# Which streams may reserve an engine, and when the dense-layer weights are loaded: a change to a list-scheduled two-layer kernel

## The chip, the cores and the metric

The kernel runs on one core of one Trainium2 chip. The metric is the time of one execution on the device in microseconds (us), as the median of several runs. The kernel before takes 727.18 us (three runs, 726.22 to 729.38). All runs compared here are of the state "fast"; the one slow run, of l_gap3, is named where it comes up. A ratio is the mean time of one kernel's fast runs over the mean of the other kernel's fast runs of the same rounds, so it is not quite the ratio of the medians quoted beside it.

Engine names: PE is TensorE, PEld its weight loads, DVE is VectorE, ACT is ScalarE, POOL is GpSimd, SP is SyncE, which here only issues DMAs.

## The reference, cut to what matters

Two layers, each an attention with a memory followed by a dense layer; 2048 tokens, width 640, 32 heads of 20, and a hidden width of 1728. The attention works in four segments of 512 tokens; each segment adds to a memory `M` that the next one reads.

```python
x = A_x
x = x + _A_ref(_layernorm(x), wq, wk, wv, wo, beta)   # attention, layer 1
x = x + _B_ref(_layernorm(x), w1, w2)                 # dense layer 1: relu(x @ w1) @ w2
x = x + _A_ref(_layernorm(x), wq, wk, wv, wo, beta)   # attention, layer 2 (same weights)
x = x + _B_ref(_layernorm(x), w1, w2)                 # dense layer 2
# in _A_ref, for each segment s and head:
#   p = softmax(q k^T * scale + causal mask);  a_dot = p v
#   a_mem = phi(q) M / (phi(q) z + 1e-6);      o = g a_mem + (1 - g) a_dot
#   M += phi(k)^T v;  z += sum phi(k)
```

## The kernel before: the parts that matter

The program is not written in its final order. Each part of the computation is a *stream*, a Python generator that yields operations. A list scheduler, run when the program is built, models each engine's time and decides the order in which each engine gets its instructions. That order is then fixed in the program, and an instruction whose input is not there yet waits on a semaphore. In the traces of before the 6344 matmuls follow, stream by stream, the order in which the scheduler put them.

```python
S.add(0, items(scores));  S.add(1, items(apply));  S.add(2, each(out_proj))
S.add(3, each(fill));     S.add(3, each(spill));   S.add(4, each(memory))
S.add(5, each(proj));     S.add(6, each(ffn))      # ffn: the dense layers, lowest compute stream
S.add(7, consts());       S.add(8, loads());       S.add(8, late_loads())
```

`scores` and `apply` treat four heads at a time; I call that a head group, 8 in a segment, 64 in all.

At each step the scheduler takes, of all streams' next operations, the one that can start first. Before that it applies a *reservation*: an operation is refused if a stream with a smaller priority number has a next operation on the same engine that could start before this one would end, beyond a tolerance.

```python
HOLD_TOL = {"pe": 220.0, "act": 150.0, "dve": 200.0, "pool": 0.0, "sp": 0.0}   # ns
...
for prio, n, st, alts in heads:                  # alts: (end, start, k, engine)
    ok = []
    for end, start, k, e in alts:
        if not any(p2 < prio and any(e2 == e and s2 + HOLD_TOL[e] < end for _, s2, _, e2 in al2[:1])
                   for p2, _, _, al2 in heads):
            ok.append((end, start, k))
```

PSUM has eight banks. Four belong to the scores (`X`, `Y`), one to apply (`OD`), and three (`MISC`) to everything else: projections, output projection, memory and dense layers. A matmul group can start only if one of the three is free; the bank comes free when an ACT or DVE operation has read it.

```python
MISC = [Slot(ps[:, 5 + k, :], "misc%d" % k) for k in range(3)]
...
def evac(n, mode, vfn, afn, waits=(), psum=True):            # reader on ACT or on DVE
    return Op([("act", (52.0 if psum else 94.0) + n / 1.2, [(afn, True)], 125.0),
               ("dve", 66.0 + n / (0.96 * mode), [(vfn, True)], 95.0)], waits)
...
def add_half(t, hf, bk, tk, waits=()):                       # residual add, DVE only
    ta = yield dve(320, 1, lambda e: e.tensor_tensor(
        x_sb[...], x_sb[...], bk.ap[:, 0:320], ALU.add), [tk] + list(waits))
    bk.release(ta)                                           # the bank comes free here
```

Q and K go through DRAM to be laid out by head: `spill` writes `scr` from `stg`, `fill` reads `pad` from `scr`. POOL issues the large loads at once:

```python
def late_loads():
    xt = yield Need("xt0")                       # first transposed activations
    ...                                          # x1, x2, x3, then wo
    z1 = yield Need("z1")
    ...                                          # w1 in one DMA of 2.2 MB, w2 in two, together 2.2 MB
```

The softmax here doesn't subtract the row's maximum and nothing guards it: scores larger than these inputs give would overflow.

Of the kernel before, what the change touches and what calls it, by code (L numbers as in the profile page):

```python
# [12 lines left out]
DH = 20  # L13
NSEG = 4
L = T // NSEG
DFF = 1728
TT = T // 128
FC = D // 128
# [6 lines left out]
NFULL = DFF // 128  # L25
# [13 lines left out]
class Prog:  # L39
# [44 lines left out]
    def dma(self, e, fn, sem):  # L84
        self.pos[e] += 1
        self.dcnt[id(sem)] = self.dcnt.get(id(sem), 0) + 16
        tk = (sem, self.dcnt[id(sem)])
        self.ops[e].append(("op", fn, sem, 16))
        self.info[(id(sem), tk[1])] = ("dma%d" % id(sem), tk[1], dict(self.K[e]))
        return tk  # L90
# [53 lines left out]

SEM_NS = 60.0
PE_MARGIN = 80.0
HOLD_TOL = {"pe": 220.0, "act": 150.0, "dve": 200.0, "pool": 0.0, "sp": 0.0}


class Sched:  # L150
# [54 lines left out]
    def _alts(self, op):  # L205
# [7 lines left out]
        for k, (e, hold, fns, tail) in enumerate(op.alts):  # L213
            m = PE_MARGIN if e == "pe" else 0.0
            start = max([self.at(t) + SEM_NS + m for t in waits], default=0.0)
# [4 lines left out]
    def run(self):  # L220
        while True:
            best = None
            moved = True
            while moved:
                moved = False
                for st in self.streams:
                    had = st[2]
                    self._settle(st)
                    if st[2] is not had and not isinstance(st[2], Op):
                        moved = moved or st[2] is None  # L230
            heads = [(st[0], n, st, self._alts(st[2])) for n, st in enumerate(self.streams)
                     if not st[4] and isinstance(st[2], Op)]
            for prio, n, st, alts in heads:
                ok = []
                for end, start, k, e in alts:
                    if not any(p2 < prio and any(e2 == e and s2 + HOLD_TOL[e] < end for _, s2, _, e2 in al2[:1])
                               for p2, _, _, al2 in heads):
                        ok.append((end, start, k))
                if not ok:
                    continue  # L240
                end, start, k = min(ok)
                key = (round(start), prio, n)
                if best is None or key < best[0]:
                    best = (key, st, end, start, k)
            if best is None:
                stuck = [st for st in self.streams if not st[4]]
                if not stuck:
                    return
                raise RuntimeError("stuck: " + "; ".join(
                    str(getattr(st[2], "key", None) or [s.name for s in st[2].slots][:2]) for st in stuck))  # L250
            _, st, end, start, k = best
            op = st[2]
            e, hold, fns, tail = op.alts[k]
            waits, slot = op.waits, None
            if op.acq is not None:
                slot = self._pick(op.acq)
                slot.free = False
                waits = waits + slot.tks
                fns = [(lambda eng, fn=fn, slot=slot: fn(eng, slot), mark) for fn, mark in fns]
            self.P.waits(e, waits)  # L260
            self.free[e] = end
            if op.dma is not None:
                tk = self.P.dma(e, fns[0][0], op.dma)
                self.dma_free[e] = max(self.dma_free[e], end) + tail[1]
                self.t[(id(tk[0]), tk[1])] = self.dma_free[e] + tail[0]
                out = tk
            else:
                marks = []
                for fn, mark in fns:
                    tk = self.P.op(e, fn, mark)  # L270
                    if tk is not None:
                        self.t[(id(tk[0]), tk[1])] = end + tail
                        marks.append(tk)
                out = marks[0] if len(marks) == 1 else (marks or None)
            st[2], st[3] = None, ((slot, out) if slot is not None else out,)
# [31 lines left out]
def bass_interleave_layers__memory_aug_infini_attn__dense_activation_relu__prompt_kernel(  # L307
    nc, A_x, A_wq, A_wk, A_wv, A_wo, A_beta, B_x, B_w1, B_w2, out,
):
    with contextlib.ExitStack() as es:  # L310
        sb = lambda name, shape, dtype=dt.bfloat16: es.enter_context(nc.sbuf_tensor(name, shape, dtype))
        sem_ = lambda name: es.enter_context(nc.semaphore(name))
        P = Prog({e: sem_("clk_" + e) for e in ["act", "dve", "pool", "pe"]})
        S = Sched(P)
# [7 lines left out]
        w1_r = sb("w1_r", [128, FC, DFFP])  # L322
        w2_r = sb("w2_r", [128, NDC, D])
# [9 lines left out]
        x_sb = sb("x_sb", [128, TT, D])  # L333
# [29 lines left out]
        pad_sem = {id(s): sem_("pad%d" % k) for k, s in enumerate(PAD)}  # L363
        scr = nc.dram_tensor("scr", [2, D + 12, 2 * L], dt.bfloat16, kind="Internal").ap()
        scr_sem = [[sem_("scr%d_%d" % (n, c)) for c in range(FC)] for n in range(2)]
# [17 lines left out]
        def ld(e, name, nbytes, fn, waits=()):  # L383
            tk = yield dma(e, sem_("d_" + name), nbytes, fn, waits)
            S.set(name, tks=[tk])

        def wload(e, name, w, src, waits=()):
            yield from ld(e, name, 819200, lambda eng: eng.dma_start(
                w[:], src.rearrange("(c p) d -> p c d", p=128)), waits)

        xs = A_x[0].rearrange("(t p) d -> p t d", p=128)
# [7 lines left out]
            yield from wload("sp", "wv", wv_r, A_wv)  # L399

        def late_loads():
            xt = yield Need("xt0")
            for s in range(1, NSEG):
                yield from ld("pool", "x%d" % s, 655360, lambda e, s=s: e.dma_start(
                    x_sb[:, 4 * s:4 * s + 4, :], xs[:, 4 * s:4 * s + 4, :]), xt if s == 1 else [])
            yield from wload("pool", "wo", wo_r, A_wo)
            z1 = yield Need("z1")
            yield from ld("pool", "w1", 2211840, lambda e: e.dma_start(
                w1_r[:, :, 0:DFF], B_w1.rearrange("(c p) f -> p c f", p=128)), z1)
            s2 = sem_("d_w2")  # L410
            yield dma("pool", s2, 2129920, lambda e: e.dma_start(
                w2_r[:, 0:NFULL, :], B_w2[0:NFULL * 128, :].rearrange("(c p) d -> p c d", p=128)))
            tk = yield dma("pool", s2, 81920, lambda e: e.dma_start(
                w2_r[0:DFF - NFULL * 128, NFULL, :], B_w2[NFULL * 128:DFF, :]), z1)
            S.set("w2", tks=[tk])
# [164 lines left out]
        def spill(a, s):  # L580
            for c in range(FC):
                ev = yield Need("stg", a, s, c)
                before = S.events.get(("filled", a, s - 2) if s > 1 else ("filled", a - 1, s + 2), [])
                tk = yield dma("sp", scr_sem[s % 2][c], 262144, lambda e, c=c: e.dma_start(
                    scr[s % 2, 128 * c:128 * c + 128, :], stg[:, c].rearrange("p n t -> p (n t)")),
                    ev + before, issue=700.0)
                S.set("packed", a, s, c, tks=[tk])

        def fill(a, s):
            got = []  # L590
            for g in range(G):
                sl = yield Acq(PAD)
                w = yield Need("z2")
                w = list(w)
                for c in range(80 * g // 128, min(FC - 1, (80 * g + 91) // 128) + 1):
                    t = yield Need("packed", a, s, c)
                    w += t
                row = scr[s % 2, 80 * g:80 * g + 1, :]
                tk = yield dma("sp", pad_sem[id(sl)], 262144, lambda e, sl=sl, row=row: e.dma_start(
                    sl.ap.rearrange("p n t -> p (n t)"),  # L600
                    bass.AP(tensor=row.tensor, offset=row.offset,
                            ap=[[DH * 2 * L, 4], [2 * L, 32], [1, 2 * L]])), w + sl.tks, issue=800.0)
                S.set("pad", a, s, g, tks=[sl, tk])
                got.append(tk)
            S.set("filled", a, s, tks=got)
# [277 lines left out]
        S.add(1, items(apply))  # L883
        S.add(2, each(out_proj))
        S.add(3, each(fill))
        S.add(3, each(spill))
        S.add(4, each(memory))
        S.add(5, each(proj))
        S.add(6, each(ffn))
        S.add(7, consts())  # L890
        S.add(8, loads())
        S.add(8, late_loads())
        S.run()
        P.waits("sp", [S.last])
# [31 lines left out]
```

## Time and profile before

| stretch, us | 0–46 | 46–120 | 120–300 | 300–480 | 480–640 | 640–722 |
|---|---|---|---|---|---|---|
| PE idle, us (length minus PE busy) | 34.4 | 19.9 | 15.3 | 17.0 | 20.2 | 4.9 |

The page's first and second part, for the kernel before. The first line gives busy time, share of the span and number of instructions. In the rows below each digit is a tenth of busy time (or of the granted TensorE clock) in one of 40 equal slices:

```profile
PE 610.5 (85%) x6344; PEld 340.6 (47%) x6344; DVE 399.6 (55%) x1178; ACT 427.5 (59%) x599; POOL 175.1 (24%) x278
PE   0644968988889999798998989897699897999998
...
PEclk9966976999999999999999889998799999999999
DMA  5958226255425233630237401255012430040201
```

The windows view, for the three middle stretches; the first number after the stretch is its length, then each engine's busy time with its number of instructions, then granted clock, DMA share and GB/s:

```profile
120.00:300.00 180.00, 164.74 (x1935) 89.48 (x1934) 121.39 (x365) 138.57 (x197) 55.25 (x86) 0.99 0.40 85
300.00:480.00 180.00, 163.05 (x1738) 90.66 (x1735) 104.80 (x299) 122.21 (x168) 50.21 (x79) 0.94 0.29 66
480.00:640.00 160.00, 139.85 (x1503) 79.67 (x1504) 91.20 (x262) 87.56 (x120) 35.93 (x57) 0.93 0.29 61
```

PE is the busiest engine, and it has one long hole at the start. The chain that ended last (start, length, what) shows a slow spill and a very slow fill, and the timeline of PE shows that PE waited for that fill:

```profile
23.70 7.46 DMA scr<-stg
31.18 14.98 DMA pad<-scr
```

```profile
29.56 1.03 PE L469 MATMUL ps<-xnT,wk_r 128*128 128x512 bf16 x4
46.21 0.61 PE L733 MATMUL ps<-pad 20*128 20x512 bf16 x4 [15.62 <-DMA pad<-scr]
```

In 28–44 us the DMA engines' share is 0.98: POOL issued about 7 MB at 19–25 us.

Here is the timeline of PE and then of DVE near 505 us, at the end of a segment:

```profile
504.96 0.34 PE L645 MATMUL ps<-BD,stg 128*128 128x147 bf16 x3
511.17 0.50 PE L645 MATMUL ps<-BD,stg 128*128 128x84 bf16 x3 [5.87 <-DVE o_sb L657]
```

### The profile page before, as it was taken

The page shows a single profiled execution, that of the slowest core. Times are in us where ns is not written, and L with a number is a line of the kernel's source. Part 1 is how long each engine was busy: PE and PEld are TensorE (multiplying, and loading weights), DVE is VectorE, ACT ScalarE, POOL GpSimd, SP SyncE. Part 2 cuts the span into 40 slices and gives each one's busy share as a digit, 9 for nine tenths or more (in the row PEclk, how much of TensorE's full clock was granted, in tenths as well). Part 3 has the DMA queues.
Part 4 walks back from the last instruction along what each step waited for, and adds up shares of the span by engine and source line. Part 5 has one row for each costly group of instructions (what it writes and reads, how often), then busy time and mean ns, then how long its engine had stood idle before and what let it go on. Part 6 is the DMA issues. An engine that isn't in the chain of part 4 may idle for free.

```text
span 722.3 us, 15107 instructions
## 1 busy us (share of the span) xinstructions
PE 610.5 (85%) x6344; PEld 340.6 (47%) x6344; DVE 399.6 (55%) x1178; ACT 427.5 (59%) x599; POOL 175.1 (24%) x278
## 2 busy tenths in 40 slices
PE   0644968988889999798998989897699897999998
PEld 0223444443445644365445554354444455465645
DVE  5116486778668484346756566365764576434102
ACT  0326895888678678666897367680287756603140
POOL 0503332323323333223333123130132223200000
PEclk9966976999999999999999889998799999999999
DMA  5958226255425233630237401255012430040201
GB/s 164 365 210 136 83 98 136 74 114 99 112 76 80 26 49 122 103 74 5 38 112 125 65 1 39 95 107 99 1 37 104 95 76 19 11 92 18 60 15 37
DMA packets 99244, 60.90 MB, mean 84 GB/s; under 512 B 80040, under 2 KB 84568, under 8 KB 99176
## 3 DMA queue, kind: packets, MB, share of 16 engines
q1 hardware_dynamic: 97552, 52.67, 31.9%
q0 software_dynamic: 1408, 7.21, 2.7%
q8 instruction: 50, 0.82, 0.5%
q14 instruction: 18, 0.15, 0.1%
q10 hardware_dynamic: 216, 0.06, 0.0%
HBM read 27.11 MB, written 13.16 MB: 56 GB/s over the span
## 4 chain that ended last, share of the span: by engine, by line
PE 62%; DMA 17%; DVE 12%; ACT 7%; issue 1%; SPq 0%
PE ps L469 40%; PE ps L466 9%; DMA scr<-stg 8%; PE ps L733 6%; PE ps L768 6%; ACT PT L740 5%; DMA pad<-scr 3%; DMA phk<-phs 3%; DVE stats L477 2%; PE ps L687 2%; DMA oT<-o_sb 1%; DVE o_sb L657 1%; DMA xnT<-xn_tok 1%; DVE x_sb L802 1%; ACT stg L554 1%
## 5 line engine op out<-in xcount | busy, mean ns | idle before, releaser
L740 ACT ACTIVATE PT<-ps 128x1024 bf16<-128x1024 f32 (+1 forms) x384 | 317.9, 882 | 164.5 <-PE ps L733 163.9
L747 POOL TENSOR_SCALAR_AFFINE_SELECT PT<-PT 128x512 bf16<-128x512 bf16 x256 | 164.3, 654 | 433.7 <-ACT PT L740 433.7
L469 PE MATMUL ps<-w_r,hT 128*128 128x320 bf16 x832 | 137.2, 306 | 0.0
L802 DVE TENSOR_TENSOR x_sb<-x_sb,ps 128x320 bf16<-128x320 bf16 x128 | 61.2, 484 | 126.1 <-PE ps L469 126.0
L469 PE MATMUL ps<-xnT,w_r 128*128 128x512 bf16 x448 | 128.0, 382 | 0.0
L733 PE MATMUL ps<-pad 20*128 20x512 bf16 (+3 forms) x1024 | 72.4, 315 | 44.7 <-ACT PT L740 26.5
L469 PEld LDWEIGHTS ps<-w_r,hT 128*128 128x128 bf16 x832 | 80.7, 100 | 34.5 <-issue 3.3
L847 ACT ACTIVATE hT<-ps 128x512 bf16<-128x512 f32 x79 | 46.8, 600 | 59.5 <-PE ps L469 59.1
L768 PEld LDWEIGHTS ps<-v_aug,PT 128*128 128x128 bf16 x2560 | 73.7, 97 | 12.1 <-POOL PT L747 3.1
L768 PE MATMUL ps<-v_aug,PT 128*128 128x21 bf16 x2560 | 75.0, 173 | 1.5 <-issue 0.4
L733 PEld LDWEIGHTS ps<-pad 20*128 20x128 bf16 x1024 | 20.8, 92 | 108.0 <-ACT PT L740 41.6
L469 PEld LDWEIGHTS ps<-xnT,w_r 128*128 128x128 bf16 x448 | 43.1, 98 | 44.3 <-issue 3.0
L477 DVE BATCH_NORM_STATS2 stats<-x_sb 128x6 f32<-128x320 bf16 x128 | 54.5, 466 | 4.5 <-DMA x_sb<-in_A_x_dram 4.5
L469 PE MATMUL ps<-wo_r,oT 128*128 128x320 bf16 x256 | 50.9, 313 | 0.0
L554 ACT ACTIVATE stg<-ps 128x512 bf16<-128x512 f32 x51 | 30.5, 601 | 33.7 <-PE ps L469 33.5
L469 PE MATMUL ps<-wv_r,xnT 128*128 128x320 bf16 x256 | 48.3, 305 | 0.0
L469 PE MATMUL ps<-xnT,wq_r 128*128 128x512 bf16 x160 | 46.9, 407 | 0.0
L466 PE MATMUL ps<-xnT,w_r 128*128 128x512 bf16 x112 | 42.9, 383 | 4.0 <-issue 1.1
L469 PE MATMUL ps<-xnT,wk_r 128*128 128x512 bf16 x160 | 45.8, 395 | 0.0
L777 DVE RECIPROCAL rden<-ps 128x16 f32<-128x16 f32 x64 | 16.2, 253 | 50.8 <-PE ps L768 50.4
L627 ACT ACTIVATE stg<-stg 128x512 bf16<-128x512 bf16 x60 | 38.3, 638 | 9.4 <-DVE rtmp L625 9.2
L625 DVE TENSOR_SCALAR rtmp<-stg 128x512 bf16<-128x512 bf16 x60 | 22.5, 375 | 35.8 <-DMA scr<-stg 35.8
(65 smaller groups left out, 565.8 us busy)
## 6 DMA issues: line engine op xcount, KB each, us to landing
pad<-scr SPq DMA_DIRECT2D x64, 256.0 KB
scr<-stg SPq DMA_DIRECT2D x40, 256.0 KB, 4.3
out_dram<-x_sb SPq DMA_DIRECT2D x16, 160.0 KB, 1.8
w_r<-in_B_w_dram POOLq DMA_DIRECT2D x1, 2160.0 KB, 15.0
w_r<-in_B_w_dram POOLq DMA_DIRECT2D x1, 2080.0 KB, 20.0
x_sb<-in_A_x_dram POOLq DMA_DIRECT2D x3, 640.0 KB, 6.6
wk_r<-in_A_wk_dram SPq DMA_DIRECT2D x1, 800.0 KB, 7.3
wq_r<-in_A_wq_dram SPq DMA_DIRECT2D x1, 800.0 KB, 8.9
```

Of the source, the lines that this page charges most:

```text
L466: bk, tk = yield pe(mm_ns(n), [(lambda e, bk, a=a, b=b: e.matmul(bk.ap[:, 0:n] if len(b.shape) == 2 else bk.ap[:, 0:n].rearrange("p (i n) ...
L469: tk = yield pe(mm_ns(n), [(lambda e, k=k, a=a, b=b, bk=bk: e.matmul(bk.ap[:, 0:n] if len(b.shape) == 2 else bk.ap[:, 0:n].rearrange("p (i ...
L477: tk = yield dve(320, 1, lambda e, c2=c2: e.bn_stats(stats6[:, t, c2, :], x_sb[:, t, c2 * 320:(c2 + 1) * 320]), xt)
L554: lambda e, sg=sg, bk=bk: e.activation(sg.ap, bk.ap[:, :], ACT.Copy),
L625: tr = yield dve(512, 4, lambda e, rt=rt, q=q: e.tensor_scalar(rt.ap, q, 0.0, 1.0, ALU.max, ALU.add), p + rt.tks)
L627: te = yield act(512, lambda e, q=q: e.activation(q, q, ACT.Exp), [tr] + p, psum=False)
L733: fns.append((lambda e, j=j, hh=hh, N=N, o=o: e.matmul(ps[:, hh, o:o + N], sl.ap[32 * hh:32 * hh + DH, 0, 128 * j:128 * j + 128], sl.ap[32 ...
L740: tx = yield act(2 * w, lambda e, k=k, bkp=bkp, u=u, w=w: e.activation(pt.ap[:, 2 * k:2 * k + 2, PT_AT[u]:PT_AT[u] + w], bkp.ap[:, :, 0:w] ...
L747: tm = yield pool(600.0, lambda e, reg=reg: e.affine_select(out=reg, in_=reg, pattern=[[0, 4], [1, 128]], compare_op=ALU.is_ge, fill=0.0, ...
L768: fns.append((lambda e, i=i, hh=hh, j=j: e.matmul(od[:, i, hh, :], pt.ap[:, hh, PT_OFF[j] + 128 * (i - j):PT_OFF[j] + 128 * (i - j) + 128] ...
L802: ta = yield dve(320, 1, lambda e: e.tensor_tensor(x_sb[:, t, 320 * hf:320 * hf + 320], x_sb[:, t, 320 * hf:320 * hf + 320], bk.ap[:, 0:32 ...
L847: lambda e, dc=dc, bk=bk: e.activation(hT[:, dc, :], bk.ap[:, :], ACT.Relu), [tk] + HT.tks)
```

## The change: intent and diff

The description says that the scheduler "reserves engines only for scores and apply" and that the dense-layer weights are loaded "in pieces behind the first heads' progress". There are three parts. I name them H (holders), L (loads) and D (the modelled cost of spill and fill DMAs).

```diff
+HOLDERS = 1                                                                  # H
-                    if not any(p2 < prio and any(...
+                    if not any(p2 < min(prio, HOLDERS) and any(...

         def late_loads():                                                    # L (cut)
-            ... x1, x2, x3, wo, w1 and w2 one behind the other after xt0
+            w = yield Need("xt0");          yield from x_load(1, w)
+            w = yield Need("filled", 0, 0); yield from x_load(2, w)
             yield from wload("pool", "wo", wo_r, A_wo)
+            for k in range(FC):             # five pieces of w1
+                w = yield Need("o", k)      # head group k is done
+                tk = yield dma("pool", s1, 442368, ... B_w1[128 * k:128 * k + 128, :]), w + z1)
+            yield from x_load(3, [])
+            for n, kn in ((5, 4), (6, 8), (7, NFULL)):      # w2 behind head groups 5 to 7
+                w = yield Need("o", n)
+                yield dma("pool", s2, 163840 * (kn - k), ...)

-    spill: dma("sp", ..., 262144, ..., issue=700.0)                          # D
+    spill: dma("sp", ..., 400000, ..., issue=350.0)
-    fill:  dma("sp", ..., 262144, ..., issue=800.0)
+    fill:  dma("sp", ..., 400000, ..., issue=550.0)
```

With `HOLDERS = 1` only priority 0, the scores, reserves; the words "and apply" would need 2. The byte counts in D are only the scheduler's figures; the DMAs move what they moved before.

More of the change, by code (lines that the diff above doesn't have):

```diff
@@ L235, in run @@
                 for end, start, k, e in alts:
-                    if not any(p2 < prio and any(e2 == e and s2 + HOLD_TOL[e] < end for _, s2, _, e2 in al2[:1])
+                    if not any(p2 < min(prio, HOLDERS) and any(e2 == e and s2 + HOLD_TOL[e] < end for _, s2, _, e2 in al2[:1])
                                for p2, _, _, al2 in heads):
@@ L401, in late_loads, with x_load @@
         def late_loads():
-            xt = yield Need("xt0")
-            for s in range(1, NSEG):
-                yield from ld("pool", "x%d" % s, 655360, lambda e, s=s: e.dma_start(
-                    x_sb[:, 4 * s:4 * s + 4, :], xs[:, 4 * s:4 * s + 4, :]), xt if s == 1 else [])
+            def x_load(s, w):
+                yield from ld("pool", "x%d" % s, 655360, lambda e: e.dma_start(
+                    x_sb[:, 4 * s:4 * s + 4, :], xs[:, 4 * s:4 * s + 4, :]), w)
+            w = yield Need("xt0")
+            yield from x_load(1, w)
+            w = yield Need("filled", 0, 0)
+            yield from x_load(2, w)
             yield from wload("pool", "wo", wo_r, A_wo)
             z1 = yield Need("z1")
-            yield from ld("pool", "w1", 2211840, lambda e: e.dma_start(
-                w1_r[:, :, 0:DFF], B_w1.rearrange("(c p) f -> p c f", p=128)), z1)
-            s2 = sem_("d_w2")
-            yield dma("pool", s2, 2129920, lambda e: e.dma_start(
-                w2_r[:, 0:NFULL, :], B_w2[0:NFULL * 128, :].rearrange("(c p) d -> p c d", p=128)))
+            s1, s2 = sem_("d_w1"), sem_("d_w2")
+            for k in range(FC):
+                w = yield Need("o", k)
+                tk = yield dma("pool", s1, 442368, lambda e, k=k: e.dma_start(
+                    w1_r[:, k, 0:DFF], B_w1[128 * k:128 * k + 128, :]), w + z1)
+            S.set("w1", tks=[tk])
+            yield from x_load(3, [])
+            k = 0
+            for n, kn in ((5, 4), (6, 8), (7, NFULL)):
+                w = yield Need("o", n)
+                yield dma("pool", s2, 163840 * (kn - k), lambda e, k=k, kn=kn: e.dma_start(
+                    w2_r[:, k:kn, :], B_w2[128 * k:128 * kn, :].rearrange("(c p) d -> p c d", p=128)), w)
+                k = kn
             tk = yield dma("pool", s2, 81920, lambda e: e.dma_start(
@@ L583, in spill @@
                 before = S.events.get(("filled", a, s - 2) if s > 1 else ("filled", a - 1, s + 2), [])
-                tk = yield dma("sp", scr_sem[s % 2][c], 262144, lambda e, c=c: e.dma_start(
+                tk = yield dma("sp", scr_sem[s % 2][c], 400000, lambda e, c=c: e.dma_start(
                     scr[s % 2, 128 * c:128 * c + 128, :], stg[:, c].rearrange("p n t -> p (n t)")),
-                    ev + before, issue=700.0)
+                    ev + before, issue=350.0)
                 S.set("packed", a, s, c, tks=[tk])
@@ L598, in fill @@
                 row = scr[s % 2, 80 * g:80 * g + 1, :]
-                tk = yield dma("sp", pad_sem[id(sl)], 262144, lambda e, sl=sl, row=row: e.dma_start(
+                tk = yield dma("sp", pad_sem[id(sl)], 400000, lambda e, sl=sl, row=row: e.dma_start(
                     sl.ap.rearrange("p n t -> p (n t)"),
                     bass.AP(tensor=row.tensor, offset=row.offset,
-                            ap=[[DH * 2 * L, 4], [2 * L, 32], [1, 2 * L]])), w + sl.tks, issue=800.0)
+                            ap=[[DH * 2 * L, 4], [2 * L, 32], [1, 2 * L]])), w + sl.tks, issue=550.0)
                 S.set("pad", a, s, g, tks=[sl, tk])
```

## The prediction

> **What bounds the kernel now.** The page shows a span of 722.3 us with PE busy 610.5 us (85%), ACT 59%, DVE 55%, POOL 24%; the chain that ended last is 62% PE, 17% DMA. By stretches (the windows view) PE is idle 34 us of the first 46, 20 of 46–120, 15 of 120–300, 17 of 300–480, 20 of 480–640, and 5 in the tail 640–722, which is dense layer only.
>
> The largest reachable hole is at the start. After the first projections PE stops at 30.6 and resumes at 46.2 us: the timeline gives 15.6 us "<- DMA pad<-scr". The chain shows why: the first spill (scr<-stg) takes 7.46 us from 23.70, the first fill (pad<-scr) 14.98 us from 31.18. The DMA view's median for a spill is 4.3 us. In 20–43 us the DMA share is 1.0 at 340–420 GB/s, because POOL issued at 19–25 us all remaining x, wo, w1 and w2 (about 7 MB). The Trainium skill ("DMA: Bandwidth & Descriptors", "Issuing engines are not separate DMA queues") says that DMAs of all issuers share 16 engines and interleave; this trace agrees. The first dense-layer matmul runs only at 153 us: 4.3 MB came 100 us too early.
>
> **What the change does.**
> 1. Loads: only x1 (0.65 MB) stays ahead of the first spill; x2 and wo wait for the first segment's fills, w1 comes in five pieces behind heads 0–4, w2 behind heads 5–7. First spill about 3.5–4.5 us, first fill about 4: scores start at 31–34 us instead of 46. PE then has work at once (V projection, last Q chunk: 8 us at 46.8–55.6). Gain about 13 us. Also the clock: 0.50 in 36–48 us; the skill ("TensorE: Matmul & The Clock Gate", Part 1) tells of a half-rate state after idle windows. About 1 us more.
> 2. Cost: about 8 more POOL DMA issues of 0.6–1.1 us (trace: 0.58–1.15) among the masks (0.65 us each), POOL 24% busy: at most 1–2 us. w1/w2 now share the DMA engines with fills and transposes at 60–110 us, where the phk transpose already takes 11.2 us: 0–4 us lost.
> 3. Scheduler: with HOLDERS = 1 only priority 0, the scores, reserves an engine (the title's "and apply" does not follow from p2 < 1). PE operations hardly change (their length, about 216 ns, is under the 220 ns tolerance); lower work fills DVE, ACT and SP earlier, apply's DVE steps may come up to 0.5 us late, with about 8.9 us per head group to absorb that. The model's spill and fill issue (700/800 to 350/550 ns) now fits the trace (326/532 ns), and longer transfers push dependent PE work later, which should shorten in-order stalls on oT (8.6 us), phk (8.4 us) and DVE. I estimate 0–8 us gain, give or take 5 us.
>
> **Critical path.** PE has a nearly fixed sum of work, and leftover dense work sits in the tail, so idle removed at the start reaches the end almost whole. Sum: −13 −1 +3 −5 and about −4 of steadier filling: 707 us, range 696–719.
>
> **What would show it.** Right: DMA share well under 1 in 28–43 us; first score matmul by 34 us; PE idle of 0–46 us down by 10 or more; POOL issues spread to about 110 us; first dense matmul 10 us earlier; tail unchanged. Wrong: the first fill still above 8 us; new PE waits on w1/w2 or on masks; longer phk and fill transfers at 60–120 us; more idle after 120 us.
>
> **What would make it wrong.** In-order engines: POOL waiting for late o events delays masks; the new order losing more in mid-kernel than 13 us.

## More of the kernel before

Layer-norms belong to the stream that needs them: the one before a dense layer to `out_proj` (priority 2), the one before a projection to `proj` (5).

A stream offers one operation at a time, so while its next operation is refused, nothing behind it in that stream is offered either.

```profile
504.42 0.49 DVE L802 TENSOR_TENSOR x_sb<-x_sb,ps 128x320 bf16<-128x320 bf16 x1 [0.28 <-PE ps L469]
504.82 0.88 DVE L477 BATCH_NORM_STATS2 stats<-x_sb 128x6 f32<-128x320 bf16 x2
505.62 0.16 DVE L654 TENSOR_SCALAR rmem<-ps 128x16 f32<-128x16 f32 x1
...
508.95 0.17 DVE L487 TENSOR_SCALAR lnU<-mv 128x4 f32<-128x4 f32 x1
...
510.63 0.48 DVE L657 TENSOR_TENSOR o_sb<-ps,rmem 128x320 bf16<-128x320 f32 x1
...
514.62 0.48 DVE L802 TENSOR_TENSOR x_sb<-x_sb,ps 128x320 bf16<-128x320 bf16 x1
```

A dense-layer matmul group ended at about 505.0 us and its bank waited until 514.6 us for the residual add. Until 510.7 us DVE did a whole layer-norm of priority 2: eight `BATCH_NORM_STATS2`, then a chain of ten or so tiny dependent steps; after that came steps of memory and apply (priorities 4 and 1). A memory reader of another bank waited too, until 510.6 us. PE started nothing from 505.3 us until that reader had freed its bank.

## The result, and the profile after

The kernel after takes 686.74 us (median of three, 684.72 to 686.8) against 727.18. The ratio is 0.943, 95% interval 0.9387 to 0.9472. It is outside the forecast range: 20 us faster than forecast, with a gain of 40 us where 20 were forecast.

The same views of the kernel after:

```profile
PE 597.6 (87%) x6344; PEld 335.3 (49%) x6344; DVE 394.6 (58%) x1191; ACT 422.6 (62%) x586; POOL 179.2 (26%) x284
PE   0863953889998999999999999977998799999998
...
PEclk9985885899999999999999999998999999999999
DMA  5568459542661515280424502564023810050201
```

```profile
120.00:300.00 180.00, 169.68 (x1972) 93.15 (x1969) 124.77 (x385) 137.15 (x190) 56.84 (x87) 0.98 0.46 94
300.00:480.00 180.00, 170.87 (x1932) 97.36 (x1929) 113.92 (x331) 129.40 (x176) 54.03 (x84) 0.97 0.36 78
480.00:640.00 160.00, 151.74 (x1555) 86.78 (x1553) 90.22 (x273) 90.05 (x125) 35.05 (x55) 0.99 0.26 55
```

The start went as forecast. The first scores are at 33.1 us instead of 46.2, with 1.16 us of waiting instead of 15.62:

```profile
33.07 0.39 PE L747 MATMUL ps<-pad 20*128 20x512 bf16 x4 [1.16 <-DMA pad<-scr]
```

But the gain does not last. The chain that ended last in the kernel after has these pieces soon afterwards:

```profile
55.00 11.11 DMA xnT<-xn_tok
...
83.38 10.30 DMA scr<-stg
...
106.95 9.22 DMA xnT<-xn_tok
```

The transpose `xnT<-xn_tok` took 3.60 us at 112.74 us in the kernel before. POOL issued x2, wo and two pieces of w1 at 53.9 to 57.3 us, and pieces of w2 at 99 and 107 us, beside these transposes. PE busy in 0–120 us is 63.8 us after and 65.8 before (the sums of the windows view's first two stretches, 22.36 + 41.43 and 11.61 + 54.15), so PE has done no more by then: 639 matmuls against 695. The eighth head group shows the same: it is done at 121.4 us after, and at 113.1 us before. (The new order has a part in this lag: e_hold_dma below, with the order of after and the loads of before, has it at 117.9 us.) So the 40 us come from elsewhere: PE idle in the three middle stretches fell from 52.4 to 27.7 us, and the dense layers of layer 1 end at 492 us instead of 525.

Idle time is not the whole gain. Of the 37.3 us between the two spans (722.3 and 685.0), PE idle over the whole span gives 24.4 us (111.8 to 87.4), and PE busy time gives 12.9 us (610.5 to 597.6) for the same 6344 matmuls, with the mean granted clock up from 0.931 to 0.948.

At the end of a segment the DVE timeline of the kernel after looks different. The residual adds (L816) and the memory readers (L671) stand between the steps of the layer-norm, and PE's longest wait there is 1.12 us (last line):

```profile
481.54 0.88 DVE L491 BATCH_NORM_STATS2 stats<-x_sb 128x6 f32<-128x320 bf16 x2
482.33 0.16 DVE L668 TENSOR_SCALAR rmem<-ps 128x16 f32<-128x16 f32 x1
482.41 0.48 DVE L816 TENSOR_TENSOR x_sb<-x_sb,ps 128x320 bf16<-128x320 bf16 x1
...
484.66 0.47 DVE L671 TENSOR_TENSOR o_sb<-ps,rmem 128x320 bf16<-128x320 f32 x1
...
485.99 0.48 DVE L816 TENSOR_TENSOR x_sb<-x_sb,ps 128x320 bf16<-128x320 bf16 x1
...
487.34 0.17 DVE L503 TENSOR_SCALAR rstd<-lnTmp 128x4 int32<-128x4 int32 x1
487.42 0.25 DVE L670 RECIPROCAL rmem<-rmem 128x16 f32<-128x16 f32 x1
487.59 0.12 DVE L505 SCALAR_TENSOR_TENSOR lnTmp<-rstd 128x4 f32<-128x4 f32 x1
487.62 0.48 DVE L816 TENSOR_TENSOR x_sb<-x_sb,ps 128x320 bf16<-128x320 bf16 x1
...
485.19 0.31 PE L480 MATMUL ps<-w_r,hT 128*128 128x320 bf16 x1 [1.12 <-DVE o_sb L671]
```

### The profile page after: what moved, and what is told of

It reads as the page before. It is cut to its first block, busy times and chain, and to the rows that moved or that the text cites. A ratio compares the mean times of both kernels' runs of the same rounds, so it can differ in the third digit from the quotient of the medians.

```text
span 685.0 us, 15109 instructions
## 1 busy us (share of the span) xinstructions
PE 597.6 (87%) x6344; PEld 335.3 (49%) x6344; DVE 394.6 (58%) x1191; ACT 422.6 (62%) x586; POOL 179.2 (26%) x284
## 4 chain that ended last, share of the span: by engine, by line
PE 67%; DMA 18%; DVE 12%; SPq 1%; ACT 1%; issue 1%
PE ps L483 43%; PE ps L480 9%; DMA scr<-stg 7%; PE ps L782 7%; PE ps L747 6%; DMA xnT<-xn_tok 4%; DMA oT<-o_sb 3%; DVE stats L491 3%; DMA phk<-phs 1%; DVE xn_tok L533 1%; DMA pad<-scr 1%; PE ps L701 1%; DVE o_sb L671 1%; PE ps L659 1%; DMA x_sb<-in_A_x_dram 1%
## 5 line engine op out<-in xcount | busy, mean ns | idle before, releaser
L483 PE MATMUL ps<-w_r,hT 128*128 128x320 bf16 x832 | 139.1, 303 | 0.0
L816 DVE TENSOR_TENSOR x_sb<-x_sb,ps 128x320 bf16<-128x320 bf16 x128 | 61.8, 484 | 107.0 <-PE ps L483 106.4
L483 PEld LDWEIGHTS ps<-w_r,hT 128*128 128x128 bf16 x832 | 79.0, 98 | 32.8 <-issue 4.1
L782 PEld LDWEIGHTS ps<-v_aug,PT 128*128 128x128 bf16 x2560 | 73.7, 96 | 11.3 <-POOL PT L761 2.6
L861 ACT ACTIVATE hT<-ps 128x512 bf16<-128x512 f32 x76 | 45.1, 598 | 53.8 <-PE ps L483 53.0
L483 PE MATMUL ps<-wo_r,oT 128*128 128x320 bf16 x256 | 49.2, 306 | 0.0
L480 PE MATMUL ps<-xnT,wk_r 128*128 128x512 bf16 x40 | 16.2, 404 | 36.7 <-DMA xnT<-xn_tok 35.0
L641 ACT ACTIVATE stg<-stg 128x512 bf16<-128x512 bf16 x60 | 38.0, 634 | 15.3 <-DVE rtmp L639 15.2
L483 PE MATMUL ps<-xnT,wk_r 128*128 128x512 bf16 x160 | 46.5, 401 | 0.0
L568 ACT ACTIVATE stg<-ps 128x512 bf16<-128x512 f32 x43 | 25.6, 599 | 33.4 <-PE ps L483 32.4
```

The lines of the kernel that those rows point to most:

```text
L480: bk, tk = yield pe(mm_ns(n), [(lambda e, bk, a=a, b=b: e.matmul(bk.ap[:, 0:n] if len(b.shape) == 2 else bk.ap[:, 0:n].rearrange("p (i n) ...
L483: tk = yield pe(mm_ns(n), [(lambda e, k=k, a=a, b=b, bk=bk: e.matmul(bk.ap[:, 0:n] if len(b.shape) == 2 else bk.ap[:, 0:n].rearrange("p (i ...
L568: lambda e, sg=sg, bk=bk: e.activation(sg.ap, bk.ap[:, :], ACT.Copy),
L641: te = yield act(512, lambda e, q=q: e.activation(q, q, ACT.Exp), [tr] + p, psum=False)
L782: fns.append((lambda e, i=i, hh=hh, j=j: e.matmul(od[:, i, hh, :], pt.ap[:, hh, PT_OFF[j] + 128 * (i - j):PT_OFF[j] + 128 * (i - j) + 128] ...
L816: ta = yield dve(320, 1, lambda e: e.tensor_tensor(x_sb[:, t, 320 * hf:320 * hf + 320], x_sb[:, t, 320 * hf:320 * hf + 320], bk.ap[:, 0:32 ...
```

## The experiments

Seventeen kernels were run besides before and after. The theories, named as in the expectations:

- A: the prediction's. The loads' gain at the start reaches the end; the scheduler part is small.
- B: the loads' gain is lost by 120 us to transposes and spills that now share the DMA engines with the weights; the gain is the new order in mid-kernel.
- C: how the order gains: a refused PSUM reader keeps a bank, so matmuls that would fill PE's holes cannot start.
- D (as a theory): the gain is ACT and DVE time saved in general, whichever operation was refused.
- E: the dense layers of layer 1 are the long pole, because as the lowest compute stream they were refused by everyone.

Two measures are worked out from the traces in the same way for all kernels. *Add wait* is the time from the (modelled) end of the last matmul of a group that ends in a residual add to the start of that add, averaged over the groups that end before 600 us; the nth group is paired with the nth add. *ReLU wait* is the same for the ReLU after the first dense matmul. *PE idle* is length minus PE busy from 120 us to the end of the last head group (its last matmul).

| kernel | median us | ratio to before | add wait / ReLU wait, us | PE idle, us |
|---|---|---|---|---|
| before | 725.7 to 728.4 | 1 | 0.76 / 0.59 | 51.7 |
| e_load (L) | 728.21 | 1.0037 | 0.74 / 0.58 | 51.7 |
| e_dma (D) | 725.51 | 0.9995 | 0.68 / 0.54 | 52.8 |
| e_hold (H) | 691.77 | 0.9521 | 0.24 / 0.26 | 29.5 |
| e_hold_dma (H+D) | 679.67 | 0.9368 | 0.29 / 0.26 | 26.2 |
| after (H+D+L) | 686.74 | 0.943 | 0.27 / 0.26 | 27.0 |
| x_evac | 697.85 | 0.9608 | 0.20 / 0.40 | 34.7 |
| x_rest | 734.25 | 1.0125 | 0.77 / 0.46 | 59.8 |
| h_dve | 709.15 | 0.9766 | 0.34 / 0.47 | 41.4 |
| h_act | 730.83 | 1.0075 | 0.67 / 0.57 | 54.4 |
| t_250 | 707.77 | 0.9741 | 0.32 / 0.52 | 46.6 |
| hn_2 | 691.06 | 0.9519 | 0.33 / 0.26 | 32.2 |
| h_jit100 | 697.06 | 0.9572 | 0.22 / 0.27 | 31.5 |
| hd_issue | 709.47 | 0.9756 | 0.19 / 0.48 | 41.7 |
| p_ffn | 740.96 | 1.0201 | 0.12 / 0.06 | 53.2 |

### 1. Each part alone, and H+D without L

A comparison of the built programs helps here. L does not change the order of a single instruction on PE, ACT, DVE or SP; it only moves POOL's DMA issues. So e_load against before, and after against e_hold_dma, show the loads alone. H and D do change the order.

**e_load**: the edit is part L of the diff above, on the kernel before.

> Only the late loads, on the kernel before. PE, ACT, DVE and SP run exactly the order of before (built programs compared); only POOL's DMA issues move. Theory A (the prediction's: the start gain reaches the end): about 712 us. Theory B (the loads' start gain is handed back by 120 us to transposes and spills that now share the DMA engines with w1, as the trace of after suggests): 722 to 730 us, with the second head about 14 us earlier than before and the eighth head not earlier.

Measured 728.21 us, ratio 1.0037 (0.9987 to 1.0088): the loads gain nothing. The first scores come at 33.4 us, but by the eighth head group the lead over before is 4.5 us (108.6 against 113.1), and at the tenth it is a lag of 5.2 us (137.0 against 131.8). The profile of e_load is of its slowest run (732.85 us), so these leads are rough; the ratio is of all its runs. Theory B holds, A falls.

**e_hold**: the edit is part H on the kernel before.

> Only HOLDERS = 1, on the kernel before (all loads early as before). Theory A: 720 to 727 us, a small effect. Theory B (the gain is the new order in mid-kernel): 695 to 705 us, with the idle time of PE between 120 and 640 us down by 15 us or more.

Measured 691.77 us, ratio 0.9521 (0.9479 to 0.9562), more than theory B forecast. This one part gives some 35 of the 40 us. Its middle stretches, to compare with before's 164.74, 163.05 and 139.85:

```profile
120.00:300.00 180.00, 171.86 (x1971) 95.53 (x1972) 126.31 (x384) 137.74 (x193) 54.70 (x87) 0.99 0.42 97
300.00:480.00 180.00, 167.15 (x1879) 94.34 (x1877) 111.87 (x328) 126.01 (x171) 51.53 (x83) 0.96 0.35 74
480.00:640.00 160.00, 150.81 (x1528) 84.68 (x1528) 88.43 (x268) 90.85 (x126) 35.22 (x56) 0.97 0.24 52
```

**e_dma**: the edit is part D on the kernel before.

> Only the scheduler's figures for the spill and fill DMAs (issue 350 and 550 ns, 400000 modelled bytes), on the kernel before. Theory A: 720 to 727 us. Theory B leaves open whether this or HOLDERS makes the mid-kernel gain; if it is this, 695 to 710 us, otherwise 718 to 730.

Measured 725.51 us, ratio 0.9995 (0.9942 to 1.0047). D reorders about a quarter of PE's operations and the time does not move.

**e_hold_dma**: parts H and D, loads early as before.

> Both scheduler parts without the late loads: the same order on PE, ACT, DVE and SP as in the kernel after, with all loads early as in before. Theory A: about 702 us (after plus the 14 us of the start). Theory B: 684 to 690 us, the same as after within 1%, because what is gained at the start is lost by 120 us.

Measured 679.67 us, below both forecasts, ratio 0.9368 (0.9317 to 0.942), while after has 0.943 (0.9387 to 0.9472). With the same order on four engines the early loads are not slower than the late ones; they look 0.7% faster, though the two intervals overlap a little and the runs were not made together. So L gives nothing at best, and D, worth nothing alone, seems to give 12 us on top of H. The second point is taken up again in part 4.

### 2. Which refused operations cost the time

**x_evac**: the reservations of before stay, except for operations of projections, output projection and dense layers that read a `MISC` bank and free it.

```diff
-if not any(p2 < prio and any(...
+if not any(p2 < (min(prio, HOLDERS) if st[2].ev else prio) and any(...
 # ev is True for evac() (projection copies, ReLU) and for add_half(); HOLDERS = 1
```

> Kernel before, with the reservations kept for all operations except those that read a bank of the three-bank PSUM pool and so free it (projection copies, ReLU, residual adds): these are refused only for the scores. Theory C (a refused PSUM reader keeps a bank, so the filler matmuls that would plug PE's holes cannot start): most of the gain of HOLDERS = 1, so 690 to 703 us, and a mean wait from the last matmul of a residual-add group to its add near 0.3 us (0.76 in before, 0.24 with HOLDERS = 1). Rival D (the gain is ACT and DVE time saved in general, whichever operation was refused): about half, 705 to 718 us.

**x_rest**: the complement, `if not st[2].ev`. The memory stream also has readers of `MISC` banks; they are not marked `ev`, so they stay refused in x_evac and go free in x_rest, whose expectation calls them operations that free no bank.

> The complement: only the operations that do not free a bank of that pool (layer-norm, memory, apply, transposes) are let off the reservations. Theory C: 715 to 728 us, with the wait before the residual adds still above 0.6 us. Rival D: about half of the gain, 705 to 715 us.

Letting through only the PSUM readers of projections, output projection and dense layers gave 697.85 us (0.9608, 0.9569 to 0.9648), which is 82% of what H gives ((1 − 0.9608) / (1 − 0.9521)). Letting through everything else gave 734.25 us (1.0125), slower than before and above theory C's forecast. The add wait followed: 0.20 us in the first, 0.77 in the second. This rules out theory D: refusing these readers is what costs the time. PE's waits fit theory C's idea of missing filler. From 120 us to the last head group, PE stood at a scores matmul waiting for an exponential of ACT (`PE ps <- ACT PT` in the waits view) for 15.1 us in 17 waits in before, for 4.4 us in x_evac, and for 0.5 us in one wait in e_hold.

What these runs do not show is theory C's reason, the bank. A refused reader keeps its bank, but it also stops its own stream, bank or no bank, and no run separates the two. The scheduler's model can be asked without the chip, by running the scheduler of each kernel with the chip's calls left empty; its latest modelled end is 658.2 us for before and 624.3 for e_hold. With before's reservations and eight `MISC` banks in place of three it is 649.5. With three banks, but a stream that goes on while its refused reader waits, it is 629.5. These are figures of the model and no times of the chip, but they put the larger part on the stopped stream and the smaller on the bank.

The Trainium skill ("Perfetto Trace Analysis", "Optimization Strategy") says that consistent bubbles on the engine that should be saturated can mean that there is not enough SBUF or PSUM for the next tile. The case agrees in kind, PE's idle being 51.7 us before and 34.7 in x_evac, but no bank was added here: the same three, with their readers let through sooner, left less idle.

**h_dve** and **h_act**: H only for operations on DVE, and only for operations on ACT.

```diff
-if not any(p2 < prio and any(...
+if not any(p2 < (min(prio, HOLDERS) if e in FREED else prio) and any(...   # FREED = ("dve",) / ("act",)
```

> HOLDERS = 1 only for operations on DVE; ACT, PE, SP and POOL keep all reservations of before. (Freeing PE, SP or POOL alone gives a program that is identical to before, so those three need no run.) Theory C with DVE as the place, since the residual adds run only there: 690 to 703 us. If ACT is the place: 718 to 728.

> HOLDERS = 1 only for operations on ACT. Theory C with DVE as the place: 718 to 728 us. If ACT is the place: 690 to 703 us.

Freeing PE, SP or POOL alone gives the identical program, so those were not run. DVE alone gave 709.15 us (0.9766), about half, and less than I expected; ACT alone 730.83 us (1.0075), no gain. So DVE is where it starts, but the two halves do not add up: both together give 0.9521. One explanation, which no run tests, is that ReLUs and copies have an alternative on each engine, so freeing one engine alone shifts the load onto it.

**t_250**: one number.

```diff
-HOLD_TOL = {..., "dve": 200.0, ...}
+HOLD_TOL = {..., "dve": 250.0, ...}
```

> One number on the kernel before: the reservation's tolerance on DVE, 200 to 250 ns. In the scheduler's model a residual add lasts 399 ns and the next step of a dependent DVE chain can start 155 ns after the last one ended, so with 200 (or 240, whose built program is all but identical to before) the add is refused at every step of such a chain, and with 250 (155 + 250 = 405) it is let in. Theory C: the wait before the residual adds falls from 0.76 us to under 0.5 and the time to 700 to 718 us. Rival D (time of ACT and DVE lost in general): under 1%, 720 to 728 us.

Measured 707.77 us, ratio 0.9741 (0.9684 to 0.9797), with the add wait down to 0.32 us. Nothing was removed here: 50 ns more of tolerance let a modelled 399 ns residual add in behind a chain whose next step the model puts at 155 ns. At 240 ns, which was not run, the scheduled order is all but that of before (35 of PE's 3296 operations are out of place in a comparison of the two orders); at 250 ns it is 1163.

**hn_2**: `HOLDERS = 2`, the change's title taken at its word.

> HOLDERS = 2 on the kernel before: scores and apply both reserve, as the change's title has it, where the diff's HOLDERS = 1 lets only the scores reserve. Theory C with the long layer-norm and memory chains (priorities 2 to 5) as the reservers: near HOLDERS = 1, 690 to 703 us. If apply's DVE steps (priority 1) are the reservers that matter: 710 to 728 us.

Measured 691.06 us (0.9519), the same as H. Apply's reservations cost nothing; those of priorities 2 and up did. The difference between title and diff does not matter for the time.

### 3. What eats the loads' gain

These kernels have H and D, and on PE, ACT, DVE and SP exactly the order of after; only POOL's issues differ.

**l_gap**: x2, wo and w1 wait until the second segment's K and Q projections have been copied out, x3 and w2 until head groups 9 to 11.

```diff
-for k in range(FC): w = yield Need("o", k) ...              # w1
+for k in range(FC): w = yield Need("stg", 0, 1, k) ...      # x2 with k = 0, wo with k = 2
-for n, kn in ((5, 4), (6, 8), (7, NFULL)): ...              # w2
+for n, kn in ((9, 4), (10, 8), (11, NFULL)): ...            # x3 with n = 9
```

> The kernel after with other gates for the late loads alone: x2, wo and w1 behind the second segment's K and Q projections (after its xnT transposes have landed), x3 and w2 behind heads 9 to 11 (after the third segment's transposes). PE, ACT, DVE and SP run exactly the order of after and of the run with both scheduler parts and early loads; only POOL's issues differ. Theory B (after loses its start gain because x2, wo, w1 and w2 share the DMA engines with the transposes at 45 to 66 and 104 to 128 us): 668 to 678 us, below both (686.7 and 679.7), with the two slow xnT transposes (11.1 and 9.2 us in after) back under 6 us. If the start gain is lost for another reason: 679 to 690 us.

Measured 680.67 us, ratio 0.9368 (0.9305 to 0.9431). The forecast of 668 to 678 was missed. The `xnT` transposes fell as expected: the third segment's to 4.60 us (9.22 in after), the second's to 4.4 (11.1). But the chain that ended last now has two spills of 10 us, at the time at which w1 comes in:

```profile
70.13 10.55 DMA scr<-stg
81.30 10.46 DMA scr<-stg
```

Only the first can be laid to w1. In l_none below, with the same gates and no w1, that spill took 5.3 us from issue to landing, but the next one still 9.9 us.

**l_none**: wrong result. w1 and w2 are never loaded, the dense matmuls read wq and wv; x2, wo and x3 have the gates of l_gap.

```diff
-(w1_r[:, k, dc * 128:(dc + 1) * 128], feat(xt, k))
+(wq_r[:, k, dc % FC * 128:(dc % FC + 1) * 128], feat(xt, k))       # and wv_r for w2_r
-    tk = yield dma("pool", s1, 442368, ...)                         # and the w2 DMAs
```

> Wrong result on purpose: w1 and w2 are never loaded, the dense layers read wq and wv in their place; x2, wo and x3 behind the same gates as in the run with other gates. PE, ACT, DVE and SP run the order of after. It measures the cost of the w1 and w2 traffic by itself. Theory B (the start gain is kept unless w1 and w2 get in the way): 662 to 670 us. If spills, fills and transposes of the second and third segment are slow without that traffic too: 675 to 682 us. No verdict on the version, only on the cost.

Measured 672.05 us, ratio 0.9255 (0.92 to 0.931). Against l_gap (0.9368), which differs only in the weight traffic, this is 1.1 points, about 8 us; against after (0.943), whose gates for x2, wo and x3 also differ, 1.75 points, about 13 us. The tenth head group is done at 123.4 us here, at 140.5 in after, at 129.4 in l_gap and at 134.7 in e_hold_dma. The time lies between the two forecasts: most of the start's gain can be kept without this traffic, but not all: one slow spill is left (9.80 us in its chain). The only load near it, wo, lands about 2 us after this spill is issued, so what slows it stays open. The Trainium skill ("DMA: Bandwidth & Descriptors", "Issuing engines are not separate DMA queues") says that DMAs of all issuers run on the same 16 engines and interleave; these runs agree for the transposes, of which the third segment's last took 9.2 us beside POOL's loads in after and 4.6 without them in l_none. The traffic has to go somewhere before the first dense layer at about 153 us, and until then there is nearly always a spill, a fill or a transpose that something waits for.

**l_gap3**: x2 and three pieces of w1 when the second segment's `xnT` has landed, wo and two pieces after its last fill, the rest as in l_gap.

> After with the loads in two gaps between DMA bursts: x2 and three pieces of w1 when the second segment's xnT has landed, wo and two pieces when its last fill has been issued and landed, x3 and w2 behind heads 9 to 11. Same order on PE, ACT, DVE and SP as after. Theory B: 668 to 677 us, below the 679.7 and 680.7 of the runs with the same order. If these gaps are no better: 679 to 687 us.

Measured 684.09 us as the median of four runs, of which one was slow (696.16); the three fast ones lie between 680.84 and 687.12 and give the ratio 0.938 (0.9329 to 0.9431). No better than l_gap. Of the kernels with a correct result e_hold_dma and l_gap are the fastest; after was not run beside them.

### 4. Is the rest, D on top of H, an effect of those figures?

**hd_issue**: H with the new issue times and the old modelled bytes. **h_jit100**: a control, H with another scheduler constant that has nothing to do with the question.

```diff
 # hd_issue: only issue=700 -> 350 (spill) and issue=800 -> 550 (fill)
 # h_jit100:
-PE_MARGIN = 80.0
+PE_MARGIN = 100.0
```

> HOLDERS = 1 with the new issue times (350, 550 ns) but the old modelled bytes. HOLDERS = 1 alone took 691.8 us, with issue and bytes 679.7. If the issue times matter: 678 to 684. If the longer modelled transfers matter: 688 to 694.

> A control: HOLDERS = 1 with the scheduler's PE_MARGIN at 100 instead of 80 ns, a change without a purpose that reorders about as many rows as the DMA figures do (823 of 1454 rows of PE differ). It shows how far an arbitrary new order moves the time. If it stays within 3 us of 691.8, the 12 us of the DMA figures are an effect of those figures; if it lies at 680 to 686 or above 698, 12 us are within what any reordering does.

hd_issue took 709.47 us (0.9756), outside both of its forecasts: 17 to 18 us slower than H alone, by ratio and by median. h_jit100 took 697.06 us (0.9572), 4 to 5 us slower than H; the two intervals overlap, and the time lies between the two bands of its expectation, so the control alone decides nothing. The add wait of hd_issue is shorter than that of H (0.19 us against 0.24), but its ReLU wait is longer (0.48 against 0.26). Its PE timeline also shows an order that fits badly, a wait for transposes of 10.5 us, where the longest such wait in H alone is 6.9 us:

```profile
472.92 0.39 PE L734 MATMUL ps<-pad 20*128 20x512 bf16 x4
483.84 0.45 PE L467 MATMUL ps<-wo_r,oT 128*128 128x320 bf16 x1 [10.53 <-DMA oT<-o_sb]
```

PE idle in hd_issue is 12.2 us above that of H, so this one wait may be much of the difference. But the three kernels with a ReLU wait near 0.5 us among those with a short add wait (h_dve, t_250, hd_issue) all took 708 to 709 us, so it need not be chance alone; no run settles this.

So other orders moved the time by 4 to 18 us once the readers are let through. Both of these made H slower and D made it faster, but the 12 us of D on top of H lie within that size, and I cannot put them down to those figures. H itself does not lie within it: the orders in which the DVE readers are let through (e_hold, hn_2, x_evac, h_jit100, e_hold_dma, h_dve, t_250, hd_issue) took 680 to 709 us, and those that still refuse the residual adds (before, e_load, e_dma, h_act, x_rest) 725 to 734 us. The exception is p_ffn_gap below, where the dense stream itself was moved.

### 5. A theory that fell: the dense layers as the long pole

In 16 kernels (all so far but l_none) the time was the end of layer 1's last dense segment plus 192 to 201 us: 525.1 and 722.3 us in before, 491.9 and 688.3 in e_hold, 534.5 and 733.3 in x_rest. That looks like a long pole. **p_ffn** tests it by moving the dense stream up, on the kernel before with all its reservations; **p_ffn_gap** does the same on l_gap.

```diff
-S.add(6, each(ffn))
+S.add(1.5, each(ffn))
```

> The kernel before with all its reservations; only the dense layers' stream moves from priority 6 to 1.5, behind scores and apply, ahead of output projection, memory and projections. Theory E (the long pole is layer 1's dense chain, because as lowest of the compute streams it was refused by all others; in 16 kernels so far the time is the end of that chain plus 192 to 201 us): the chain ends at 485 to 500 us instead of 525 and the time is 685 to 703 us. Rival C alone (banks held too long, whoever holds them): the dense stream no longer waits but now refuses the others' readers, so 710 to 735 us.

> The same move of the dense stream on top of both scheduler parts and the load gates of l_gap (680.7 us without the move). An attempt at a faster version. Theory E: the reservations no longer hold the dense stream there, so little is left: 670 to 683 us. If the higher priority starves the attention of layer 2 instead: above 686.

p_ffn took 740.96 us, ratio 1.0201 (1.0152 to 1.0249); p_ffn_gap 730.29 us (1.0063), 50 us slower than l_gap. In p_ffn layer 1's dense part ended at 434 us, 91 us earlier than before, and the rest then took 310 us. So it was no long pole, and theory E falls: in the 16 kernels the end of that part was a mark of how well PE had been filled until then. The run also bounds theory C, whose forecast of 710 to 735 us it missed. With add and ReLU waits of 0.12 and 0.06 us, shorter than in any other row of the table, PE was idle for 53.2 us. Short waits are not enough by themselves. A plausible reading is that the dense matmuls are worth most as filler: started only when nothing better is ready, but allowed to finish and free their bank at once. Moved ahead of the others they are used up early, and the attention that follows lacks them. That reading fits p_ffn, where PE's waits at scores for an exponential are back at 15.2 us in 14 waits (120 us to the last head group), but I did not isolate it.

## Why the prediction was wrong, point by point

- *The start*: right. It forecast first scores at 31–34 us (33.1), a DMA share well under 1 in 28–43 us (0.37 in 28–44, from 0.98), and PE idle of 0–46 us down by 10 or more (34.4 to 23.6). The granted clock of 28–44 us went from 0.65 to 1.00; the Trainium skill ("TensorE: Matmul & The Clock Gate", Part 1) tells of a half-rate state after idle windows, and the stretch 36–48 us of before, granted 0.50 after PE had stopped, agrees.
- *"Idle removed at the start reaches the end almost whole"*: wrong. The loads alone gave a ratio of 1.0037. The error was in a term that I had named: "w1/w2 now share the DMA engines with fills and transposes at 60–110 us ... 0–4 us lost". The w1 and w2 traffic measured about 8 us (l_none against l_gap), and 13 us against after, where x2, wo and x3 come at other times too; that is about the forecast gain of 14 us. What the loads slowed, as far as the runs show, are the `xnT` transposes of the second and third segment: 6.6 to 11.3 us from issue to landing in after, 3.4 to 4.4 in before. Nor was PE's sum of work fixed: it was busy for 610.5 us in before and 597.6 in after.
- *"Scheduler ... 0–8 us gain, give or take 5 us"*: this is the step that failed most. It measured 35 us for `HOLDERS = 1` alone. I had checked PE's operations against PE's tolerance (right: freeing PE alone changes nothing) and stopped there. I did note that lower work would fill DVE and ACT earlier, but took that as filling engines that are only 55 to 59% busy. I did not ask what an operation refused on DVE holds up meanwhile: one of three PSUM banks and the rest of its own stream, so PE's filler. In before the wait for the residual add averaged 0.76 us with single waits up to 9.7 us; with H it averaged 0.24. The scheduler's own model would have told the size without the chip: its latest modelled end is 658.2 us for before, 624.3 with H, 658.4 with D, and 658.2 with L, which it does not see. The two errors had opposite signs: the start's 14 us came to about nothing, and the scheduler part, forecast as 9 us (5 and 4), to 35.
- *Apply's DVE steps up to 0.5 us later, absorbed*: consistent. Whether apply reserves or not makes no difference (hn_2 and e_hold).
- *The DMA figures shorten in-order stalls on oT and phk*: not shown. Alone they changed the time by −0.05%. PE's waits went from 8.6 us on oT and 8.4 on phk in before to 8.2 and 6.5 in after.
- *First dense matmul 10 us earlier; tail unchanged*: both wrong. It came at 159.9 us instead of 153.2, and the time from the last head group to the end fell from 93 to 81 us.
- *POOL issues spread to about 110 us, masks not a problem*: right in kind (the last issue is at 124 us); PE's list of waits shows nothing on masks worth naming.
- *"Reordering may go either way by 5 us"*: too small. One reordering of H, hd_issue, moved the time by 17 to 18 us.

What stays open: why D on top of H gave 12 us, and how much of H's gain comes from filler becoming available and how much from other effects of the new order, and, on the chip, how much of the filler was kept back by a held bank and how much by a stopped stream.

## What to carry to other kernels

In a list scheduler that reserves engines by priority, look at what a refused operation holds up while it is refused: if it frees a scarce buffer of the busiest engine, or if its stream offers nothing further until it is done, refusing it for the sake of a small step on a half-idle engine can cost the busy engine its filler. Ask the scheduler's own model before the chip: here it told the size of H (34 us modelled, 35 measured), though not the differences among the orders with H (626.1 us modelled for h_dve and 625.7 for hd_issue, both near 709 measured). Moving a load out of one collision is worth only what the next collision leaves of it; run the load change alone, with the order of the instructions unchanged, before counting its gain. And with in-order engines keep a control that reorders without a purpose: here it and a partial edit moved the time by 4 to 5 and 17 to 18 us, so smaller gains of a scheduling constant should not be explained.

## What the Trainium skill lacked or had wrong

- "DMA: Bandwidth & Descriptors", "Anatomy of one DMA — SWDGE (gpsimd) path", fits a DMA issued from POOL at about 2.0 us plus bytes / 436e3. For w1's 2.2 MB in one piece that gives 7.1 us, and for a 442 KB piece 3.0 us (both are estimates worked out from that fit). The profile page shows, from issue to landing, 15.0 us in before and a median of 6.6 us in after, both beside other DMAs. The fit holds no term for other traffic, and a kernel that loads while it computes needs one.
- The same page, "DMA Transpose (X-bar)" and the rules for kernel authors, says of correctness what may run beside a transpose, but gives no time for one beside other traffic. The runs show 3.6 us for `xnT<-xn_tok` in the chain of before, and 11.1 and 9.2 us in after beside loads from POOL.
- "Perfetto Trace Analysis", "Optimization Strategy", names too little PSUM as a reason for bubbles. It does not name the case here: the same banks, freed late because the reader stands behind unrelated work in another engine's order. Changing which readers may go first, with the same three banks, took PE's idle from 51.7 to 34.7 us (x_evac).
- No page that I read says how far an arbitrary new order on in-order engines moves the time. Here it was 4 to 5 us, not clear of noise, for a scheduler constant without bearing on the question, and 17 to 18 us for a partial edit (h_jit100 and hd_issue against e_hold).
